# Attention followed by a tanhshrink FFN on one core: the conversion of the weights goes through PSUM tiles at the products with v

## The chip, the cores and the metric

The kernel runs on one core of a Trainium2 chip. The metric is device time in microseconds (us). Engines are named as in the profile: PE multiplies matrices and writes PSUM, PEld loads its weights, DVE, ACT and POOL work on elements, SP issues the DMA transfers. PSUM is the memory that PE writes its results to; SBUF is the other on-chip memory.

## The reference

The attention has 8 batches of 8 heads, 1152 positions and 64 numbers per head. The queries are averaged in twos, so 576 query rows meet 1152 keys. Its result, as 4608 tokens of 512 numbers, goes through a feed-forward network of 512 to 2048 to 512.

```python
q_pool = q.reshape(B, H, S // 2, 2, D).mean(axis=3)
scores = scale * np.matmul(q_pool, k.transpose(0, 1, 3, 2))
scores = scores - np.max(scores, axis=-1, keepdims=True)
attn = np.exp(scores)
attn = attn / (np.sum(attn, axis=-1, keepdims=True) + 1e-09)
x = np.matmul(attn, v)            # then (B, H, S, D) -> (4608, 512)
h = x @ w_in
out = (h - np.tanh(h)) @ w_out
```

q, k and v are 32-bit floats. The two weight matrices are 64-bit floats, and the kernel receives them as pairs of 32-bit words. It has to make 32-bit numbers of them before the network can use them: this is the conversion that the change is about.

## The kernel before

**Two stages.** The attention fills about the first half of the time and the network the second. The conversion of the weights is done during the attention, in 32 blocks of 128 x 512 weights, and its results go to DRAM, from where the network loads them.

**The attention.** Two heads make a pair, and there are 32 pairs. A pair takes U = 36 steps, called units, and is split in two halves of 18 units, 288 queries each. At each even unit of a half PE forms the scores of one of nine key tiles (`scores`: eight matmuls into one PSUM tile), and ACT takes the exponential out of it into a `p_f` tile. In a half's last unit PE multiplies the nine `p_f` tiles with v (`pv`, 36 matmul rows in the trace), and ACT copies the result out (`o_out`, tile `o_s`). After the products with v of the second half PE also sums the exponentials with a matrix of ones (`z_sums`, 32 rows), from `z` tiles that POOL has added up, and ACT copies that out too (`z_out`).

**The maxima.** While a pair's scores run, the row maxima of the next pair are found ahead: `max_part` has PE form 128 query rows by 384 keys for two heads, and one unit later DVE reduces them (`mx`). There are 15 of these per pair, eight in a second half and seven in a first half (counted by the half that runs beside them). At the end of a first half `max_rows` takes the maximum of these (`nm`), PE turns it (a transpose with `ident`), ACT and DVE split it in a high and a low part (`mt`), and it goes through DRAM to the rows `mb` of a matmul that subtracts it from the scores.

**High and low parts.** q and k are split too: `hi` (ACT, three instructions per pair) and `lo` (DVE, one subtraction over 128 x 1728), so that three products of parts stand for one product.

**The ring.** All PSUM tiles of the attention come from one pool of four (`banks`), each of 128 x 2 x 512 floats. A score tile, a `max_part` tile, the result of `pv` with that of `z_sums`, and the transpose each take one. PE can write a tile only when the reader of the tile that lay in that place before is done.

**The order** on each engine is the order in which the code calls it. Work that is not scores is put into tables by unit: `first` and `early` run at the start of a unit, ahead of its scores, and `at` behind its scores. In a half's last unit, `at` comes ahead of `pv`. So work in `at` of that unit and work in `first` of the next one stand on the two sides of `pv`, which matters only to PE and to what waits for PE.

**The conversion** of a block (`w_block`, called at unit 5 of a pair in the regular case) is: load (`w_raw`); ACT scales the upper words (`begin`); DVE clamps them, takes the sign, shifts and joins (three instructions); DVE takes the exponent (`w_2`), multiplies it with 16 bits of the lower word (two instructions); POOL adds; ACT makes the high part and POOL the low part (`w_hl`); SP stores. All tiles are in SBUF. The number ahead of each step is its unit behind the call.

In the profile most instructions of the attention have line L37, that of a helper that records every one of them, so they are told apart by their tiles: `w<-w` and `w<-w_raw,w` on DVE are the conversion, `mx<-ps` are the maxima, `lo<-kq,hi` is the low part.

Of the kernel before, what the change touches and what calls it, by code (L numbers as in the profile page):

```python
# [8 lines left out]
F32 = mybir.dt.float32  # L9
F32R = mybir.dt.float32r  # L10
I32 = mybir.dt.int32
# [32 lines left out]
def kernel(  # L44
# [18 lines left out]
    P = 128  # L63
# [76 lines left out]
    with ExitStack() as actx:  # L140
# [31 lines left out]
        def banks(dtype=F32):  # L172
            return ps_a.tile([P, 2, 512], dtype, name="ps")
# [173 lines left out]
        def w_block(u, kind, r, c):  # L347
# [7 lines left out]
            def begin():  # L355

                t[:] = [wp.tile([P, WB], I32, name=f"w_{i}", bufs=1 + (i < 2)) for i in range(3)]
                t.append(wp.tile([P, 2, WB], F32R, name="w_hl", bufs=2))
                act.activation(whole(t[0]), whole(hi), AF.Copy, scale=2.0 ** -112)

            def whole(x):
                return x.bitcast(F32)

            def store():
                src = t[3].bitcast(F32)
                if kind == 0:
# [3 lines left out]
                else:  # L370
                    sp.dma_start(wo_dram[r, :, :, c:c + WB], src)
            sp.dma_start(raw.rearrange("p n w -> p (n w)"),
                         (w_in, w_out)[kind][r * P:(r + 1) * P, 2 * c:2 * (c + WB)])
            for i, op in ((12, begin),
                          (30, lambda: ts(whole(t[0]), whole(t[0]), -top, top, op0=ALU.max, op1=ALU.min)),
                          (30, lambda: ts(t[1], t[0], -0x80000000, None, op0=ALU.bitwise_and)),
                          (48, lambda: stt(t[1], t[0], 3, t[1], op0=ALU.logical_shift_left, op1=ALU.bitwise_or)),
                          (48, lambda: ts(t[2], t[1], -0x800000, None, op0=ALU.bitwise_and)),
                          (48, lambda: stt(whole(t[2]), lo, 2.0 ** -36, whole(t[2]), op0=ALU.mult, op1=ALU.mult)),
                          (50, lambda: pool.tensor_tensor(whole(t[1]), whole(t[1]), whole(t[2]), op=ALU.add)),  # L380
                          (66, lambda: act.activation(t[3][:, 0], whole(t[1]), AF.Copy)),
                          (68, lambda: pool.tensor_tensor(t[3][:, 1], whole(t[1]), whole(t[3][:, 0]), op=ALU.subtract)),
                          (75, store)):
                add(u + i, op)
# [32 lines left out]
        for pi in range(n_pair):  # L417
            u = pi * U
            units = dict(load=-80, query_sums=-62, hi=-55, lo=-37, load_v=-30)
            row, steps = -19, (5, 11)  # L420
# [196 lines left out]
```

## Time and profile before

| what | value |
| --- | --- |
| median of the runs | 1643.94 us (three runs, 1643.39 to 1645.49) |
| the profiled execution | 1643.04 us |
| its span in the trace | 1641.3 us |
| TensorE clock granted | 0.999 of full speed |
| PE, DVE, ACT, POOL busy | 98%, 80%, 62%, 57% of the span |

The span is what lies between the first and the last instruction of the program; the profiled execution took 1.74 us more. A busy PE is not a PE at its peak, since matmuls overlap and their ends are modelled. Times in a timeline are from the start of the span. Each row of a timeline has the start, the time that the merged instructions took together, the engine, the line, the operation, the tiles and how many instructions were merged; in brackets stands how long the engine was idle ahead of it and what ended that wait.

### The profile page before, as it was taken

The numbers are of one execution on the slowest core, as the hardware profiler recorded it, in microseconds if no ns is written. First come the engines' busy times: TensorE is split into PE (matmuls) and PEld (weight loads), VectorE is DVE, ScalarE is ACT, GpSimd is POOL, SyncE is SP. The second block draws the span as 40 slices with busy tenths as digits, with TensorE's granted clock in tenths as the row PEclk, the third lists the DMA queues.
The fourth block names the chain that finished last, engine by engine and source line by source line (L and its number), as shares of the span: only waits on it lengthen the run. The fifth ranks groups of instructions, "written<-read, shape, count | busy, mean of one in ns | idle before, by whom it ended". The sixth has DMA issues, their size and how long they took to land.

```text
span 1641.3 us, 32231 instructions
## 1 busy us (share of the span) xinstructions
PE 1609.8 (98%) x12576; PEld 1245.2 (76%) x12576; DVE 1319.6 (80%) x1725; ACT 1023.9 (62%) x1865; POOL 942.9 (57%) x694
## 2 busy tenths in 40 slices
PE   5999999999999999999999999999999999999999
PEld 3667777777777777677778888888888888888898
DVE  7889888888898888888848677777777777777786
ACT  2655656556556565565566666666666666666786
POOL 2778778778787787877854343433434342423332
PEclk9999999999999999999999999999999999999999
DMA  3343444334433344343547110101011111000100
GB/s 141 120 138 108 126 127 136 125 108 138 135 115 125 121 141 126 108 130 133 183 146 268 39 36 21 48 26 52 26 47 31 39 39 39 26 33 20 32 22 27
DMA packets 72665, 147.86 MB, mean 90 GB/s; under 512 B 11136, under 2 KB 36672, under 8 KB 72512
## 3 DMA queue, kind: packets, MB, share of 16 engines
q1 hardware_dynamic: 72512, 145.80, 27.3%
q8 instruction: 99, 1.62, 0.4%
q14 instruction: 54, 0.44, 0.1%
HBM read 109.49 MB, written 36.27 MB: 89 GB/s over the span
## 4 chain that ended last, share of the span: by engine, by line
PE 85%; DVE 13%; issue 1%; ACT 0%; DMA 0%; DVEq 0%; ACTq 0%
PE ps L37 37%; PE ps_h L37 24%; PE ps_o L37 24%; DVE w L37 6%; DVE mx L37 6%; DVE nm L37 0%; DVE lo L37 0%; DMA q_n<-in_q_dram 0%; ACT hi L37 0%; DVE rec L37 0%; DVE kq L37 0%; ACT p_f L37 0%; DVEq L37 0%; ACT x L552 0%; ACT z_s L37 0%
## 5 line engine op out<-in xcount | busy, mean ns | idle before, releaser
L37 DVE TENSOR_REDUCE mx<-ps 128x2 f32<-128x768 f32 x480 | 434.3, 951 | 73.9 <-PE ps L37 73.7
L37 POOL TENSOR_TENSOR g_lo<-g_s,g_hi 128x512 fp32r<-128x512 f32 (+1 forms) x160 | 190.3, 1190 | 483.3 <-ACT g_hi L520 445.2
L37 ACT ACTIVATE p_f<-ps 128x576 f32<-128x576 f32 x576 | 361.7, 650 | 93.6 <-PE ps L37 79.3
L37 POOL TENSOR_TENSOR z<-p_f 128x576 f32<-128x576 f32 x192 | 280.0, 1459 | 154.1 <-ACT p_f L37 154.1
L37 PE MATMUL ps<-hi 64*128 64x288 f32 (+1 forms) x2112 | 316.7, 352 | 23.7 <-DVE mx L37 13.7
L37 PE MATMUL ps_h<-x,wi 128*128 128x512 f32 (+1 forms) x1440 | 318.3, 370 | 0.0
L37 PE MATMUL ps_o<-wo,g_hi 128*128 128x512 f32 x1008 | 311.5, 390 | 0.0
L37 PE MATMUL ps<-p_f,v 128*64 128x288 f32 x2304 | 293.5, 409 | 0.0
L37 PEld LDWEIGHTS ps_h<-x,wi 128*128 128x128 f32 x1440 | 253.1, 188 | 50.5
L37 PEld LDWEIGHTS ps<-hi 64*128 64x128 f32 x2112 | 194.4, 187 | 89.2 <-DVE mx L37 34.6
L37 PEld LDWEIGHTS ps<-p_f,v 128*64 128x64 f32 x2304 | 159.8, 137 | 113.7 <-ACT p_f L37 12.0
L509 ACT ACTIVATE g_u<-ps_h 128x512 f32<-128x512 f32 (+1 forms) x160 | 88.9, 556 | 236.3 <-PE ps_h L37 236.1
L514 DVE SCALAR_TENSOR_TENSOR ps_w<-g_u,ps_h 128x512 f32<-128x512 f32 (+1 forms) x160 | 103.1, 645 | 157.8 <-ACT g_t L510 157.2
L37 PEld LDWEIGHTS ps_o<-wo,g_hi 128*128 128x128 f32 x1008 | 187.6, 188 | 39.2
L37 POOL TENSOR_TENSOR z<-z,p_f 128x576 f32<-128x576 f32 x128 | 194.0, 1516 | 11.8 <-ACT p_f L37 1.9
L37 PE MATMUL ps_o<-wo,g_lo 128*128 128x512 f32 x504 | 196.2, 389 | 0.0
L37 PE MATMUL ps<-lo,hi 64*128 64x288 f32 x1152 | 170.8, 293 | 0.0
L37 PE MATMUL ps<-hi,lo 64*128 64x288 f32 x1152 | 170.7, 293 | 0.0
L37 PE MATMUL ps<-mb,ones_k 64*128 64x288 f32 x1152 | 170.2, 292 | 0.0
L37 ACT ACTIVATE o_s<-ps 128x288 f32<-128x288 f32 x64 | 26.3, 412 | 230.4 <-PE ps L37 230.4
L519 DVE COPY_PREDICATED g_s<-g_m,g_t 128x512 f32<-128x512 int32 (+1 forms) x160 | 115.0, 719 | 17.1 <-DVE g_s L518 0.9
L517 DVE SCALAR_TENSOR_TENSOR ps_w<-g_s,ps_w 128x512 f32<-128x512 f32 (+1 forms) x160 | 102.9, 643 | 16.6 <-DVE ps_w L516 0.5
(68 smaller groups left out, 2399.7 us busy)
## 6 DMA issues: line engine op xcount, KB each, us to landing
q_n<-in_q_dram SPq DMA_DIRECT2D x32, 576.0 KB
kq<-in_k_dram SPq DMA_DIRECT2D x32, 576.0 KB
v<-in_v_dram SPq DMA_DIRECT2D x32, 576.0 KB
x_dram<-o_s SPq DMA_DIRECT2D x32, 288.0 KB
out_dram<-o_s SPq DMA_DIRECT2D x34, 256.0 KB
w_raw<-in_moe_w_in_dram SPq DMA_DIRECT2D x16, 512.0 KB
wi_dram<-w_hl SPq DMA_DIRECT2D x16, 512.0 KB
w_raw<-in_moe_w_out_dram SPq DMA_DIRECT2D x16, 512.0 KB
```

Source lines behind the costliest of these rows:

```text
L37: ins = self.tc.keep_in_program_order(f(*args, **kwargs))
L509: nc.scalar.activation(u, h, AF.Square)
L514: nc.vector.scalar_tensor_tensor(w, u, -P0, h, op0=ALU.add, op1=ALU.mult)
L517: nc.vector.scalar_tensor_tensor(w, s2, P2, w, op0=ALU.add, op1=ALU.mult)
L519: last = nc.vector.copy_predicated(s1, m.bitcast(I32), th).ins
```

## The change

The conversion's first intermediate tile now lies in the PSUM ring instead of SBUF. `begin` on ACT writes a tile of the ring, and the clamp, the sign and the join on DVE read it; the joined word goes to the SBUF tile `w_1`. The exponent is written to a second tile of the ring (`scale`), and the multiplication with the lower word reads it from there. So each block takes two places of the ring, for a short time each. The tiles `w_0` are gone, `w_1` has three buffers instead of two, and the pair of tiles `w_hl` is taken only when the high part is made (`split`).

The steps also move. `begin`, the clamp, the sign and the join all stand in `first` of one unit, 31 behind the call: for a regular block that is the first unit of the next pair, right behind the products with v and the sums of a second half. The exponent and the multiplication stand in `first` 49 behind the call, right behind the products with v of that pair's first half. Before, `begin` stood ahead of the products with v of a first half, clamp and sign ahead of those of a second half, and join, exponent and multiplication ahead of those of the next first half. The low part `lo` moves by one unit, from the end of a second half to the first unit of the next pair, behind the scores there.

```diff
             def begin():
 
-                t[:] = [wp.tile([P, WB], I32, name=f"w_{i}", bufs=1 + (i < 2)) for i in range(3)]
-                t.append(wp.tile([P, 2, WB], F32R, name="w_hl", bufs=2))
+                t[:] = [banks(I32)[:, 0], wp.tile([P, WB], I32, name="w_1", bufs=3)]
                 act.activation(whole(t[0]), whole(hi), AF.Copy, scale=2.0 ** -112)
+
+            def scale():
+                t[0] = banks(I32)[:, 0]
+                ts(t[0], t[1], -0x800000, None, op0=ALU.bitwise_and)
+
+            def split():
+                t[0] = wp.tile([P, 2, WB], F32R, name="w_hl", bufs=2)
+                act.activation(t[0][:, 0], whole(t[1]), AF.Copy)
...
-            for i, op in ((12, begin),
-                          (30, lambda: ts(whole(t[0]), whole(t[0]), -top, top, op0=ALU.max, op1=ALU.min)),
-                          (30, lambda: ts(t[1], t[0], -0x80000000, None, op0=ALU.bitwise_and)),
-                          (48, lambda: stt(t[1], t[0], 3, t[1], op0=ALU.logical_shift_left, op1=ALU.bitwise_or)),
-                          (48, lambda: ts(t[2], t[1], -0x800000, None, op0=ALU.bitwise_and)),
-                          (48, lambda: stt(whole(t[2]), lo, 2.0 ** -36, whole(t[2]), op0=ALU.mult, op1=ALU.mult)),
-                          (50, lambda: pool.tensor_tensor(whole(t[1]), whole(t[1]), whole(t[2]), op=ALU.add)),
-                          (66, lambda: act.activation(t[3][:, 0], whole(t[1]), AF.Copy)),
-                          (68, lambda: pool.tensor_tensor(t[3][:, 1], whole(t[1]), whole(t[3][:, 0]), op=ALU.subtract)),
+
+            for i, op in ((31, begin),
+                          (31, lambda: ts(whole(t[0]), whole(t[0]), -top, top, op0=ALU.max, op1=ALU.min)),
+                          (31, lambda: ts(t[1], t[0], -0x80000000, None, op0=ALU.bitwise_and)),
+                          (31, lambda: stt(t[1], t[0], 3, t[1], op0=ALU.logical_shift_left, op1=ALU.bitwise_or)),
+                          (49, lambda: t.append(wp.tile([P, WB], I32, name="w_2", bufs=1))),
+                          (49, scale),
+                          (49, lambda: stt(whole(t[2]), lo, 2.0 ** -36, whole(t[0]), op0=ALU.mult, op1=ALU.mult))):
+                add(u + i, op, at=first)
+            for i, op in ((50, lambda: pool.tensor_tensor(whole(t[1]), whole(t[1]), whole(t[2]), op=ALU.add)),
+                          (66, split),
+                          (68, lambda: pool.tensor_tensor(t[0][:, 1], whole(t[1]), whole(t[0][:, 0]), op=ALU.subtract)),
                           (75, store)):
                 add(u + i, op)
...
-            units = dict(load=-80, query_sums=-62, hi=-55, lo=-37, load_v=-30)
+            units = dict(load=-80, query_sums=-62, hi=-55, lo=-36, load_v=-30)
```

**DVE, once around a pair.** The rows begin with the last seven maxima beside a second half and end with the maxima beside the next second half; `nm` marks the products with v of the first half. A number behind `w` is one tile of one block. Before:

```order
L37 TENSOR_REDUCE mx<-ps 128x2 x7
L37 TENSOR_TENSOR lo<-kq,hi 128x1728
L37 TENSOR_SCALAR w_2708<-w_2708 128x512
L37 TENSOR_SCALAR w_2709<-w_2708 128x512
L37 TENSOR_REDUCE mx<-ps 128x2 x7
L37 TENSOR_REDUCE nm<-mx 128x10
L37 SCALAR_TENSOR_TENSOR w_2709<-w_2708,w_2709 128x512
L37 TENSOR_SCALAR w_2710<-w_2709 128x512
L37 SCALAR_TENSOR_TENSOR w_2710<-w_raw,w_2710 128x512
L37 TENSOR_REDUCE mx<-ps 128x2
L37 TENSOR_TENSOR mt<-ps,mt 10x128
L37 TENSOR_REDUCE mx<-ps 128x2 x7
```

And with the change:

```order
L37 TENSOR_REDUCE mx<-ps 128x2 x7
L37 TENSOR_SCALAR ps<-ps 128x512
L37 TENSOR_SCALAR w_2927<-ps 128x512
L37 SCALAR_TENSOR_TENSOR w_2927<-ps,w_2927 128x512
L37 TENSOR_TENSOR lo<-kq,hi 128x1728
L37 TENSOR_REDUCE mx<-ps 128x2 x7
L37 TENSOR_REDUCE nm<-mx 128x10
L37 TENSOR_SCALAR ps<-w_2927 128x512
L37 SCALAR_TENSOR_TENSOR w_3108<-w_raw,ps 128x512
L37 TENSOR_REDUCE mx<-ps 128x2
L37 TENSOR_TENSOR mt<-ps,mt 10x128
L37 TENSOR_REDUCE mx<-ps 128x2 x7
```

The join (`w_2709<-w_2708,w_2709` before) has moved from the first half's products with v to those of the second half, and `lo` has moved behind the three instructions of the conversion. Between `nm` and the next maximum two instructions stand where there were three.

**ACT, over the same stretch.** Before:

```order
L37 ACTIVATE p_f<-ps 128x576 x8
L37 ACTIVATE w_hl<-w_2709 128x512
L37 ACTIVATE o_s<-ps 128x288
L37 ACTIVATE z_s<-ps 128x288
L37 ACTIVATE p_f<-ps 128x576 x9
L37 ACTIVATE hi<-kq 128x576 x3
L37 ACTIVATE w_3466<-w_raw 128x512
L37 ACTIVATE o_s<-ps 128x288
```

And with the change:

```order
L37 ACTIVATE p_f<-ps 128x576 x8
L37 ACTIVATE w_hl<-w_2927 128x512
L37 ACTIVATE ps<-w_raw 128x512
L37 ACTIVATE o_s<-ps 128x288
L37 ACTIVATE z_s<-ps 128x288
L37 ACTIVATE p_f<-ps 128x576 x9
L37 ACTIVATE hi<-kq 128x576 x3
L37 ACTIVATE o_s<-ps 128x288
```

`begin` (the row that reads `w_raw`) has moved from the first half's products with v to those of the second half, where DVE's next instruction now waits for it.

More of the change, by code (lines that the diff above doesn't have):

```diff
@@ L364, in store @@
             def store():
-                src = t[3].bitcast(F32)
+                src = t[0].bitcast(F32)
                 if kind == 0:
```

## The prediction

> **What bounds the kernel now.** I read the page first (busy shares, chain of waits), then the busy time by stage, then the timeline of DVE and PE around one pair, and last the pairs that are longer than the others. The chain's row by engine, and two stages of the table by windows (start and end, length, then busy us and count of PE, PEld, DVE, ACT, POOL, and the granted clock):
>
> ```profile
> PE 85%; DVE 13%; issue 1%; ACT 0%; DMA 0%; DVEq 0%; ACTq 0%
> ...
> 127.00:757.00 630.00, 625.47 (x6948) 452.25 (x6947) 559.35 (x586) 382.45 (x674) 502.40 (x324) 1.00 0.39 127
> ...
> 845.00:1641.00 796.00, 792.46 (x3647) 657.13 (x3645) 592.68 (x962) 530.81 (x996) 296.15 (x268) 1.00 0.16 51
> ```
>
> The network, from 845 us on, holds no conversion, and the change doesn't reach it. All that can move lies in the attention, where DVE is busy for 89% (559.35 of 630) and has 13% of the chain. So the question is where in a pair DVE is late. The products with v are clear marks in PE's timeline; three in a row, two of one pair and the first of the next:
>
> ```profile
> 298.76 4.59 PE L37 MATMUL ps<-p_f,v 128*64 128x288 f32 x36
> ...
> 310.75 4.59 PE L37 MATMUL ps<-p_f,v 128*64 128x288 f32 x36
> ...
> 324.00 4.59 PE L37 MATMUL ps<-p_f,v 128*64 128x288 f32 x36
> ```
>
> From the end of the first (303.35) to the second it takes 7.40 us, from the end of that (315.34) to the next pair 8.66. DVE over the same stretch:
>
> ```profile
> 299.98 0.18 DVE L37 TENSOR_REDUCE nm<-mx 128x10 f32<-128x30 f32 x1
> 300.08 0.68 DVE L37 SCALAR_TENSOR_TENSOR w<-w,w 128x512 int32<-128x512 int32 x1
> 300.87 1.45 DVE L37 TENSOR_SCALAR w<-w 128x512 int32<-128x512 int32 x1
> 302.36 1.77 DVE L37 SCALAR_TENSOR_TENSOR w<-w_raw,w 128x512 f32<-128x512 uint16 x1
> 304.05 0.94 DVE L37 TENSOR_REDUCE mx<-ps 128x2 f32<-128x768 f32 x1
> 305.41 0.28 DVE L37 TENSOR_TENSOR mt<-ps,mt 10x128 fp32r<-10x128 f32 x1 [0.41 <-ACT mt L37]
> 305.62 1.80 DVE L37 TENSOR_REDUCE mx<-ps 128x2 f32<-128x768 f32 x2
> ...
> 311.97 3.02 DVE L37 TENSOR_TENSOR lo<-kq,hi 128x1728 fp32r<-128x1728 f32 x1
> 314.91 1.96 DVE L37 TENSOR_SCALAR w<-w 128x512 f32<-128x512 f32 x2
> 317.83 0.96 DVE L37 TENSOR_REDUCE mx<-ps 128x2 f32<-128x768 f32 x1 [0.97 <-PE ps L37]
> ```
>
> The two sides differ. Beside the first half's products with v, the conversion runs until the first maximum, with no idle time between: DVE is just late. Beside the second half's, `lo` and two conversion instructions are done at 316.87, and DVE then waits 0.97 us for PE: there is slack. Behind a first half a delay is paid, behind a second half up to 0.97 us are free.
>
> How much a delay costs is seen where DVE has more to do. After each fourth pair the reciprocals of a batch stand behind the conversion; first PE, then DVE, then their count in the attention:
>
> ```profile
> 349.25 4.59 PE L37 MATMUL ps<-p_f,v 128*64 128x288 f32 x36
> ...
> 361.62 4.59 PE L37 MATMUL ps<-p_f,v 128*64 128x288 f32 x36
> ```
>
> ```profile
> 354.54 0.17 DVE L37 TENSOR_SCALAR rec<-rec 128x36 f32<-128x36 f32 x1
> 354.74 0.38 DVE L37 RECIPROCAL rec<-rec 128x36 f32<-128x36 f32 x1
> 355.04 0.90 DVE L37 TENSOR_REDUCE mx<-ps 128x2 f32<-128x768 f32 x1
> ```
>
> ```profile
> L37 DVE RECIPROCAL rec<-rec x7: 378/378/379, 152.0 to 760.2; 128x36 f32<-128x36 f32 x7
> ```
>
> Here the stretch is 361.62 - 353.84 = 7.78 us. And what it is with DVE free is seen in the first pair, where POOL happened to be idle (from 43.86, by its row), so that the conversion was quick; PE, DVE, POOL:
>
> ```profile
> 42.08 4.59 PE L37 MATMUL ps<-p_f,v 128*64 128x288 f32 x36
> ...
> 54.01 4.59 PE L37 MATMUL ps<-p_f,v 128*64 128x288 f32 x36
> ```
>
> ```profile
> 44.44 0.43 DVE L37 TENSOR_SCALAR w<-w 128x512 int32<-128x512 int32 x1
> 44.90 0.69 DVE L37 SCALAR_TENSOR_TENSOR w<-w_raw,w 128x512 f32<-128x512 uint16 x1
> 47.29 0.96 DVE L37 TENSOR_REDUCE mx<-ps 128x2 f32<-128x768 f32 x1 [1.69 <-PE ps L37]
> ```
>
> ```profile
> 45.68 1.27 POOL L37 TENSOR_TENSOR w<-w,w 128x512 f32<-128x512 f32 x1 [1.82 <-DVE w L37]
> ```
>
> DVE waited 1.69 us for PE, and the stretch was 54.01 - 46.67 = 7.34. These three numbers, 7.34, 7.40 and 7.78, are the core of the prediction. The same rows price the instructions: 0.43 and 0.69 us alone, 1.45 and 1.77 beside a busy POOL.
>
> **The change, part by part.** *First half.* Three instructions become two: the exponent into PSUM, and the multiplication that reads it from there. No conversion instruction of before touches PSUM, so their price is bounded: below by 0.43 (alone in SBUF), above by 1.77 (beside POOL). I take the nearest rows, those of the network that read and write PSUM over the same 512 elements, and for `lo` alone the row from the start of the kernel, when POOL was idle:
>
> ```profile
> L517 DVE SCALAR_TENSOR_TENSOR ps_w<-g_s,ps_w 128x512 f32<-128x512 f32 x125 | 87.1, 697 | 13.2 <-DVE ps_w L516 0.5
> ```
>
> ```profile
> 30.55 1.95 DVE L37 TENSOR_TENSOR lo<-kq,hi 128x1728 fp32r<-128x1728 f32 x1
> ```
>
> So 0.70 each, and 0.11 between two of which one needs the other (300.08 + 0.68 to 300.87). From 300.16 the two end at 301.67, with reciprocals (0.55) at 302.2, where PE's first maximum let DVE start no earlier than about 303.97 (in the first pair 0.62 us behind the products with v, 46.67 to 47.29). DVE is no longer late in either case, and every such stretch goes to 7.34. Cover: 1.8 us; if the two cost 1.45 and 1.77 as now, they end at 303.49 and regular pairs still gain, but those with reciprocals end at 304.04 and keep 0.06.
>
> A rule of the Trainium skill bears on this price, SBUF — State Buffer, section "Who interferes with whom": a DVE instruction with at most one input in SBUF, outside the two-port modes, doesn't contend with GpSimd (POOL). The trace agrees as far as it goes (0.43 and 0.69 alone against 1.45 and 1.77); by that rule the 0.70 holds beside POOL too, and the slower rival below loses its ground. Another, VectorE: DVE Perf Modes, section "Why PSUM operands drop a tier", speaks against the change: a PSUM operand loses the double rate of fp32. By it an instruction of 0.43 goes to 0.70, which over three is 0.8 us more per pair than alone. On the path that would be 24 us over 30 pairs and the change slower; against the 1.45 of now it is 2.2 less per pair, and the trace puts it under cover.
>
> *Second half.* Now three dependent conversion instructions come first and `lo` behind them, and they wait for `begin` on ACT, which is queued behind the high part `w_hl`. ACT and POOL there, the mean of `begin`, and a low part on POOL at a time when no `lo` ran:
>
> ```profile
> 311.27 0.62 ACT L37 ACTIVATE w_hl<-w 128x512 fp32r<-128x512 f32 x1
> ```
>
> ```profile
> L37 ACT ACTIVATE w<-w_raw 128x512 f32<-128x512 f32 x25 | 16.8, 673 | 0.0
> ```
>
> ```profile
> 313.12 3.00 POOL L37 TENSOR_TENSOR w_hl<-w,w_hl 128x512 fp32r<-128x512 f32 x1
> ```
>
> ```profile
> 99.45 1.46 POOL L37 TENSOR_TENSOR w_hl<-w,w_hl 128x512 fp32r<-128x512 f32 x1
> ```
>
> `begin` ends at 311.89 + 0.67 = 312.56; DVE's reductions end at about 312.05, so it waits 0.5 us. Then 3 x 0.70 + 2 x 0.11 = 2.32, to 314.88. POOL's low part, 1.46 long, is done at 314.58, so `lo` has POOL out of its way and costs 1.95: the end is 316.83, the maximum waits for PE until 317.83, and 1.0 us is spare. If `lo` still costs 3.02, the end is 317.90, 0.07 too late; over 29 pairs that is 2 us of loss. Queued behind `begin` on ACT are `o_s` and `z_s`, which need products that end 2.8 us later. I take no cost here, 0 to 2.
>
> *The ring.* Two more tiles per pair pass through four places. A place that `begin` took is free at 314.88, and one that the exponent took at 301.67; PE asks for its next score tiles only behind the products with v, after 315.34 and 303.35. Price nothing; without that cover, it would be the delay of the DVE instruction itself.
>
> *The long pairs.* Early blocks bunch up in the second and third pair. PE's marks there:
>
> ```profile
> 67.26 4.59 PE L37 MATMUL ps<-p_f,v 128*64 128x288 f32 x36
> ...
> 80.95 4.59 PE L37 MATMUL ps<-p_f,v 128*64 128x288 f32 x36
> ...
> 95.32 4.58 PE L37 MATMUL ps<-p_f,v 128*64 128x288 f32 x36
> ...
> 108.01 4.59 PE L37 MATMUL ps<-p_f,v 128*64 128x288 f32 x36
> ```
>
> The stretches are 9.10, 9.78 and 8.11 us, that is 1.76, 1.12 and 0.77 over 7.34, 8.66 and 7.34. Five conversion instructions stand at the first two, also with the change: 5 x 0.81 = 4.05 us, which fits beside 4.59 us of products only if `begin` is in time. It is behind three `hi` on ACT in the first, so I take 1.2 of 1.76; in the second 0.9 of 1.12, since `lo` follows; in the third, two instructions, all 0.77. At the start, before the first pair, the three instructions and `lo` take 2.3 + 1.95 to 3.0 us where `lo` and two slow ones take 4.95 (30.55 to 35.50): a gain of 0.7 to a loss of 0.4, taken as nothing.
>
> *The sum.* Thirty pairs have maxima beside their second half. Seven with reciprocals: 7 x 0.44 = 3.1. Three long ones: 1.2 + 0.9 + 0.77 = 2.9. The other twenty, without the first, which is at 7.34 already: 19 to 20 x 0.06 = 1.2. Together 7.2 us: 1643.04 - 7.2 = 1635.8 for a profiled execution. The median of the runs is 0.9 above that execution, so the prediction is 1636.7. From the bounds: at most 3.1 + 1.2 + 1.76 + 1.12 + 0.77 + 0.7 = 8.7; at least 3.1 + 1.2 + 0 + 0.4 + 0.77 - 2.0 - 0.4 = 3.1.
>
> DVE's work falls much more: its conversion from 1.96 + 0.68 + 1.45 + 1.77 = 5.9 to 3.5 us per pair, and `lo` by 1.1. Over 30 pairs that is 100 us, of which 7 count. Behind 7.34 and 8.66 stand PE's own matmuls and the chain of maxima, which the change doesn't shorten: 0.41 us before `mt` are a wait for ACT.
>
> **The rivals.** *Nothing follows.* The maximum at 304.05 is followed by a wait of 0.41 anyway, so its lateness might cost nothing, and the reciprocals might be paid elsewhere. Then only the long pairs gain, 2.9: 1641.0. The 7.78 next to 7.40 speaks against it.
>
> *Slower: the second half overruns.* The point is 317.83: from 312.56 there are 5.27 us for three instructions, two gaps and `lo`. With `lo` at 3.02 it decides from 0.68 per instruction on, with 1.95 from 1.03. Were PSUM to cost as much as the 768-element reduction (0.95) and POOL still to slow `lo`, the end would be 318.65, 0.8 late in 29 pairs: 23 us, against 7 gained: 1660. For it speaks that `lo` has run 3.02 beside POOL's low part; against it that POOL's would be done before.
>
> *More: a wait that vanishes.* The trace puts one kind of PE's waits ahead of a score or maximum tile on the conversion:
>
> ```profile
> PEld ps L37 <- issue: 24.3, 55, 0.5
> ...
> PEld ps L37 <- DVE w L37: 8.8, 19, 0.5
> ```
>
> If that is a true wait, 8.8 us in 25 pairs, 10 or so in all, go too: 1627. Against it: 55 + 19 are three per pair of one length, two of them called "issue", so this looks like the same gap at a change of operands.
>
> **How the numbers follow.** The forecast gets 0.78, nothing follows 0.10, slower 0.05, more 0.07. The range is 1633.5 to 1641.0: the bounds of the sum (1635.2 to 1640.8), about 1 us either way for the spread of the runs (1643.39 to 1645.49), cut at 1641.0. A measurement of this kernel can tell about 0.2%, 3.3 us, from no change, which is 1640.6. Faster: 0.78 + 0.07 = 0.85; the same: 0.10; slower: 0.05.
>
> **What would show it.** In the profile after: every regular stretch behind a first half at 7.34, also with reciprocals; an idle time ahead of the first maximum there of 1 us or more; 8.66 behind a second half; conversion instructions of 0.70, `lo` of 1.95, POOL's low part below 1.5; DVE busy about 100 us less in all. The prediction is wrong if the stretch of 8.66 grows (the first maximum of a pair without idle time ahead of it), if conversion instructions on PSUM take over 1 us, or if ACT's `o_s` or PE's first scores are late behind tiles of the ring.

## The result, and the profile after

The changed kernel takes 1635.13 us (median of five runs, 1634.2 to 1635.39); the kernel before took 1643.46 beside it (five runs, 1642.98 to 1645.49). The ratio is 0.9947, with a 95% interval of 0.9937 to 0.9958. The span of the profiled execution went from 1641.3 to 1632.4 us, and the last products with v of the attention start at 828.00 instead of 836.80: 8.8 of the 8.9 us lie in the attention.

The chain of waits by engine, and the same two stages by windows:

```profile
PE 97%; DVE 2%; ACT 0%; DMA 0%; issue 0%; ACTq 0%
...
127.00:757.00 630.00, 629.78 (x6977) 454.72 (x6975) 487.80 (x590) 383.48 (x676) 447.07 (x326) 1.00 0.40 127
845.00:1632.00 787.00, 783.62 (x3608) 650.40 (x3606) 588.01 (x955) 524.35 (x986) 295.62 (x268) 1.00 0.15 49
```

DVE is busy for 487.80 us in place of 559.35 in the attention's window, and its share of the chain is 2% instead of 13%. PE's timeline at the same pair as before, products with v only:

```profile
293.00 4.59 PE L37 MATMUL ps<-p_f,v 128*64 128x288 f32 x36
...
304.99 4.59 PE L37 MATMUL ps<-p_f,v 128*64 128x288 f32 x36
...
318.18 4.59 PE L37 MATMUL ps<-p_f,v 128*64 128x288 f32 x36
```

The stretch behind the first half is 304.99 - 297.59 = 7.40, as before; the one behind the second half 318.18 - 309.58 = 8.60, where it was 8.66. DVE's timeline over both:

```profile
298.21 0.96 DVE L37 TENSOR_REDUCE mx<-ps 128x2 f32<-128x768 f32 x1 [2.43 <-PE ps L37]
299.66 0.28 DVE L37 TENSOR_TENSOR mt<-ps,mt 10x128 fp32r<-10x128 f32 x1 [0.49 <-ACT mt L37]
...
306.72 0.70 DVE L37 TENSOR_SCALAR ps<-ps 128x512 f32<-128x512 f32 x1 [0.42 <-ACT ps L37]
307.45 0.69 DVE L37 TENSOR_SCALAR w<-ps 128x512 int32<-128x512 int32 x1
308.18 0.69 DVE L37 SCALAR_TENSOR_TENSOR w<-ps,w 128x512 int32<-128x512 int32 x1
308.78 1.95 DVE L37 TENSOR_TENSOR lo<-kq,hi 128x1728 fp32r<-128x1728 f32 x1
312.07 0.96 DVE L37 TENSOR_REDUCE mx<-ps 128x2 f32<-128x768 f32 x1 [1.34 <-PE ps L37]
```

Ahead of the first maximum DVE now idles 2.43 us behind a first half and 1.34 behind a second one. So it is late nowhere, and still the first stretch is 7.40 and not 7.34. That is the point at which the prediction failed, and most runs below are about it.

Here is where the 8.8 us came from, by the starts of all products with v. The start of the kernel: the first ones begin at 41.12 instead of 42.08, 0.96. The second pair: stretches of 7.59 and 8.61 in place of 9.11 and 9.78, 2.7. The third: 7.34 for 8.11, 0.8. The pairs with reciprocals: six go from 7.79 to 7.40 and a seventh from 8.01, 2.9. The other stretches behind second halves: 8.66 to 8.61 in nearly all, less 0.4 at two pairs that have 8.84 and 8.82, 1.4. The twenty regular stretches behind first halves: nothing.

### The profile page after: what moved, and what is told of

Same layout as the page of the kernel before. It is cut to its first block, busy times and chain, and to the rows that moved or that the text cites. A ratio compares the mean times of both kernels' runs of the same rounds, so it can differ in the third digit from the quotient of the medians.

```text
span 1632.4 us, 32106 instructions
## 1 busy us (share of the span) xinstructions
PE 1611.2 (99%) x12576; PEld 1246.3 (76%) x12576; DVE 1226.8 (75%) x1725; ACT 1023.4 (63%) x1865; POOL 873.3 (53%) x694
## 4 chain that ended last, share of the span: by engine, by line
PE 97%; DVE 2%; ACT 0%; DMA 0%; issue 0%; ACTq 0%
PE ps L37 49%; PE ps_h L37 24%; PE ps_o L37 24%; DVE mx L37 1%; DMA q_n<-in_q_dram 0%; ACT hi L37 0%; ACT p_f L37 0%; DVE lo L37 0%; DVE kq L37 0%; DVE w L37 0%; DVE ps L37 0%; ACT x L562 0%; ACT z_s L37 0%; ACT mt L37 0%; DVE nm L37 0%
## 5 line engine op out<-in xcount | busy, mean ns | idle before, releaser
L37 POOL TENSOR_TENSOR z<-p_f 128x576 f32<-128x576 f32 x192 | 275.2, 1433 | 236.7 <-ACT p_f L37 236.7
L37 POOL TENSOR_TENSOR z<-z,p_f 128x576 f32<-128x576 f32 x128 | 183.1, 1431 | 10.0
```

The lines of the kernel that those rows point to most:

```text
L37: ins = self.tc.keep_in_program_order(f(*args, **kwargs))
```

## The experiments

All runs in one table. A stretch is the time from the end of one half's products with v to the start of the next: regular pairs, pairs with reciprocals, and behind a second half. It is what most stretches of the kind have in the profiled execution; single ones differ. The ratio is to the kernel before beside the run, with its 95% interval.

| run | us | ratio | regular | reciprocals | second half |
| --- | --- | --- | --- | --- | --- |
| before | 1643.46 | | 7.40 | 7.79 | 8.67 |
| after | 1635.13 | 0.9947 (0.9937 to 0.9958) | 7.40 | 7.40 | 8.61 |
| e1_sbuf | 1640.09 | 0.998 (0.997 to 0.9989) | 7.40 | 7.40 | 8.67 |
| e2_scale | 1651.71 | 1.0047 (1.0032 to 1.0062) | 7.40 | 7.40, two of 7.63 and 7.68 | 9.05 |
| e3_lo | 1635.48 | 0.9949 (0.9934 to 0.9964) | 7.40 | 7.40 | 8.61 |
| e4_rec | 1641.01 | 0.9986 (0.9976 to 0.9995) | 7.40 | 7.40, two of 7.62 and 7.68 | 8.67 |
| e5_first | 1658.22 | 1.0083 (1.0067 to 1.0099) | 7.66 | 8.16 or 10.6 to 10.9 | 8.60 |
| e6_second | 1658.6 | 1.0091 (1.0076 to 1.0107) | 7.40 | 7.40 | 9.26 |
| e7_seen | 1632.31 | 0.9933 (0.992 to 0.9945) | 7.34 | 7.34 | 8.60 |
| e9_bseen | 1639.7 | 0.9975 (0.9964 to 0.9985) | 7.34 | 7.77 | 8.61 |
| e10_place | 1641.75 | 0.9988 (0.9979 to 0.9997) | 7.40 | 7.67, two of 7.90 and 7.94 | 8.67 |
| e8_seen2 | 1633.12 | 0.9934 (0.992 to 0.9947) | 7.34 | 7.34 | 8.61 |
| t_spot | 1634.01 | 0.9943 (0.9929 to 0.9957) | 7.38 | 7.38 | 8.60 |

### The order without PSUM, and PSUM without the order

**e1_sbuf**: the changed kernel with its two conversion tiles back in SBUF.

```diff
-                t[:] = [banks(I32)[:, 0], wp.tile([P, WB], I32, name="w_1", bufs=3)]
+                t[:] = [wp.tile([P, WB], I32, name="w_0", bufs=1), wp.tile([P, WB], I32, name="w_1", bufs=3)]
...
-                t[0] = banks(I32)[:, 0]
+                t[0] = wp.tile([P, WB], I32, name="w_3", bufs=1)
```

> The changed kernel with its order, but with both conversion tiles in SBUF again. Theory (the place counts: in PSUM the DVE instructions keep clear of POOL): beside POOL the five instructions go back to 0.7 to 1.8 us each and lo to 2 to 3 us; with three of them and lo behind the second half's products, the first maximum of a pair is late by 0 to 2.6 us, taken as 1.3, so 1635 + 29 x 1.3 = about 1673, and in any case over 1640. Rival (the new order alone makes the gain): 1635, the stretches stay at 7.40 and 8.61.

DVE's timeline in that run, from a first half's products to behind a second half's:

```profile
300.77 1.72 DVE L37 SCALAR_TENSOR_TENSOR w<-w_raw,w 128x512 f32<-128x512 uint16 x1
304.15 0.96 DVE L37 TENSOR_REDUCE mx<-ps 128x2 f32<-128x768 f32 x1 [1.65 <-PE ps L37]
...
312.68 2.37 DVE L37 TENSOR_SCALAR w<-w 128x512 f32<-128x512 f32 x2 [0.44 <-ACT w L37]
315.08 0.69 DVE L37 SCALAR_TENSOR_TENSOR w<-w,w 128x512 int32<-128x512 int32 x1
315.69 1.95 DVE L37 TENSOR_TENSOR lo<-kq,hi 128x1728 fp32r<-128x1728 f32 x1
318.01 0.96 DVE L37 TENSOR_REDUCE mx<-ps 128x2 f32<-128x768 f32 x1 [0.36 <-PE ps L37]
```

In SBUF the conversion is slower (1.72 for an instruction that takes 0.69 with PSUM), but it still fits: 1.65 and 0.36 us are idle. So neither theory held: the time is just over the 1640 of the first, but no maximum is late in a regular pair. By the medians the order alone gives 3.2 us (1643.33 beside it), mostly at the pairs with reciprocals (7.40) and at the third pair (7.40 for 8.11), and PSUM the other 5.

PSUM's part lies at the start and in the second pair, where blocks bunch up, and in 0.06 per second half. How much it is at the first two can't be read off this one execution (1641.44 us, above its kernel's median). The first products start at 42.69 against 41.12, and the second pair's stretches are 10.56 and 9.46 against 7.59 and 8.61. But in the second pair PE works at a granted clock of 0.60 for a while:

```profile
76.00:80.00 4.00, 3.92 (x36) 3.92 (x38) 2.22 (x5) 1.51 (x3) 1.88 (x2) 0.60 0.57 178
```

In the kernel before, at a clock of 1.00 there, DVE's first maximum is nearly as late (2.47 us behind the products, here 2.60), and the stretch is 9.11. So an estimated 1.3 of the 2.97 us go with the clock, and something at the start too, as told below.

**e4_rec**: the kernel before with only its reciprocals moved, from behind the conversion at a first half to the next second half.

```diff
-                    add(u + 17, lambda: reciprocals(dve, *tot[0]))
-                    add(u + 20, lambda: spread(sp, *tot.pop(0)))
+                    add(u + 35, lambda: reciprocals(dve, *tot[0]))
+                    add(u + 38, lambda: spread(sp, *tot.pop(0)))
```

> The kernel before, with the reciprocals moved from behind the first half's products to behind the second half's, where DVE waits 0.97 us for PE and they take 0.55. Theory: the stretches with reciprocals go from 7.78 to 7.40 and nothing else moves: 7 x 0.39 = 2.7 us less than before, about 1640.8. Rival (those stretches are long for another reason, such as the transfer of the sums): no change.

1641.01, with 7.40 at five of those seven pairs: as expected. (The fifth and the seventh have 7.68 and 7.62; why wasn't followed.) This prices the pairs with reciprocals by themselves. DVE is still late by about 0.1 us behind first halves: in a first half of this run the products end at 353.59 and the maximum starts 0.72 behind,

```profile
354.31 0.94 DVE L37 TENSOR_REDUCE mx<-ps 128x2 f32<-128x768 f32 x1
```

where one that waits for PE starts 0.62 behind (297.59 to 298.21 in the changed kernel). The stretch is 7.40 in both: the first 0.1 us costs nothing.

**e2_scale**: the kernel before, with only the exponent tile in PSUM; the order of the steps as before, so the tile is taken in `at`, ahead of the first half's products with v.

```diff
+            def scale():
+                t.append(banks(I32)[:, 0])
+                ts(t[4], t[1], -0x800000, None, op0=ALU.bitwise_and)
...
-                          (48, lambda: ts(t[2], t[1], -0x800000, None, op0=ALU.bitwise_and)),
-                          (48, lambda: stt(whole(t[2]), lo, 2.0 ** -36, whole(t[2]), op0=ALU.mult, op1=ALU.mult)),
+                          (48, scale),
+                          (48, lambda: stt(whole(t[2]), lo, 2.0 ** -36, whole(t[4]), op0=ALU.mult, op1=ALU.mult)),
```

> The kernel before, with only the exponent's tile in PSUM; order and everything else as before. Theory (the gain is the end of DVE's lateness behind a first half): the two instructions there go from 1.45 and 1.77 to 0.7 each, the seven stretches with reciprocals from 7.78 to 7.40 (2.7 us), the long third and second pairs lose 0.8 and about 1.5, the second halves stay at 8.66: about 1638.5. Rival (the second half's new order is needed for it): within 1 us of before, 1643.

It is slower than before, by 0.47%. The first halves gained about what was expected, but every stretch behind a second half grew by 0.38. PE, and DVE just ahead of it:

```profile
301.73 4.59 PE L37 MATMUL ps<-p_f,v 128*64 128x288 f32 x36 [0.32 <-DVE mx L37]
```

```profile
300.71 1.82 DVE L37 TENSOR_REDUCE mx<-ps 128x2 f32<-128x768 f32 x2 [0.33 <-PE ps L37]
```

The products with v wait for a maximum's reduction (the first of these two ends at about 301.6). With a tile of the ring taken just ahead of them, they get a place that is still held.

**e10_place** tests that reading: the same tile, but the two instructions stand in `first` of the next unit, where the change has them, so that the products take their place in the ring ahead of the exponent.

```diff
-                          (48, scale),
-                          (48, lambda: stt(whole(t[2]), lo, 2.0 ** -36, whole(t[4]), op0=ALU.mult, op1=ALU.mult)),
+            for op in (scale, lambda: stt(whole(t[2]), lo, 2.0 ** -36, whole(t[4]), op0=ALU.mult, op1=ALU.mult)):
+                add(u + 49, op, at=first)
```

> The kernel before, with the exponent tile in PSUM as in the run that was slower (ratio 1.0047), but its instruction and the multiplication behind it written in the place where the change has them, so that the tile is taken from the ring behind the products with v and not ahead of them; DVE's order stays. Theory (what cost 0.38 per pair was the place in the ring: the first half's products then took the place of a maximum that DVE had not read yet): stretches behind a second half back to 8.67, those behind the pairs with reciprocals still at 7.40; 2.5 us less than before: about 1640.8. Rival (a fifth user of the four places costs 0.38 wherever it is taken): 1651 to 1652, stretches of 9.05.

8.67 again: the 0.38 was the place in the ring. In the program, the first matmul of these products waits for DVE in the one and for ACT's exponential in the other:

```
L37 MATMUL ps<-p_f,v 64x288 [waits DVE_49]
L37 MATMUL ps<-p_f,v 64x288 [waits Activation_49]
```

The pairs with reciprocals only went to 7.67, not 7.40, so it is 0.9 us slower than expected. There the maximum isn't late (354.43 to 355.05, 0.62), but `mt` waits longer for ACT, 0.76 against 0.49 in the changed kernel.

```profile
354.28 0.69 DVE L37 SCALAR_TENSOR_TENSOR w<-w_raw,ps 128x512 f32<-128x512 uint16 x1
355.05 0.96 DVE L37 TENSOR_REDUCE mx<-ps 128x2 f32<-128x768 f32 x1
356.77 0.28 DVE L37 TENSOR_TENSOR mt<-ps,mt 10x128 fp32r<-10x128 f32 x1 [0.76 <-ACT mt L37]
```

```profile
355.02 0.18 PEld L37 LDWEIGHTS ps<-hi 64*128 64x128 f32 x2 [0.27 <-DVE w L37]
```

```profile
355.94 0.65 ACT L37 ACTIVATE p_f<-ps 128x576 f32<-128x576 f32 x1 [1.05 <-PE ps L37]
```

This is the ring again. DVE, behind the reciprocals, reads the exponent's tile until 354.28 + 0.69 = 354.97, and PE's next scores wait 0.27 us for that place. The exponential, with `mt` behind it on ACT, starts 1.51 us behind the products instead of 1.24, and the stretch is 0.27 longer. So a tile that is taken behind the products is free only while DVE is done with it in time.

**e3_lo**: the changed kernel with `lo` back at the end of the second half, ahead of the conversion.

```diff
-            units = dict(load=-80, query_sums=-62, hi=-55, lo=-36, load_v=-30)
+            units = dict(load=-80, query_sums=-62, hi=-55, lo=-37, load_v=-30)
```

> The changed kernel with the low part lo ahead of the conversion again, as before. Theory: lo runs beside POOL again and takes 2 to 3 us where it takes 1.95, and the idle time of 1.34 us ahead of a pair's first maximum shrinks by that, but stays above zero: the time stays at 1635 to 1636. Rival (lo's place is part of the gain): 1638 or more, first maxima without idle time ahead.

`lo` takes 3.0 us again, since POOL's low part runs beside it and itself takes 2.9 (1.29 on average in the changed kernel), and the stretches stay the same:

```profile
L37 DVE TENSOR_TENSOR lo<-kq,hi 128x1728 fp32r<-128x1728 f32 x32 | 94.4, 2951 | 0.0
```

```profile
L37 POOL TENSOR_TENSOR w_hl<-w,w_hl 128x512 fp32r<-128x512 f32 x32 | 92.7, 2898 | 0.0
```

So the move of `lo`, by which it takes 1.95, is worth nothing in regular pairs: that microsecond lies in DVE's slack. Only in the second pair, where two blocks meet, does it count: 9.01 for 8.61.

### How much lateness costs, on both sides

**e5_first** and **e6_second** make DVE late in the changed kernel, by repeats that don't alter the result.

```diff
-                ts(t[0], t[1], -0x800000, None, op0=ALU.bitwise_and)
+                for _ in range(5):
+                    ts(t[0], t[1], -0x800000, None, op0=ALU.bitwise_and)
```

> The changed kernel, with the exponent instruction of the conversion written five times in a row (the result is the same), so that DVE has four more instructions of about 0.77 us (0.70 and the gap), 3.08 us, ahead of the first maximum behind a first half's products with v, where it idles 2.43 us now. Theory (what DVE is late there is paid, but for a first 0.1 to 0.2 us; the late reciprocals of the kernel before, 0.59 late, cost 0.39): 0.65 late, some 0.45 per pair in 29 pairs, 13 us, and about 2.6 in the crowded second pair: about 1651, stretches of 7.85 in place of 7.40. Rival (lateness behind a first half isn't paid, and the gain at the pairs with reciprocals has another cause): 1635, stretches of 7.40.

```diff
-                          (31, lambda: ts(t[1], t[0], -0x80000000, None, op0=ALU.bitwise_and)),
+                          *[(31, lambda: ts(t[1], t[0], -0x80000000, None, op0=ALU.bitwise_and))] * 4,
```

> The changed kernel, with the sign instruction written four times in a row (the result is the same): three more of about 0.73 us, 2.19, ahead of the first maximum behind a second half's products, where DVE idles 1.34 us now. This is the price and the point of the prediction's slower rival. Theory (the second half overruns once its 1.34 are used up): 0.85 late, 0.65 to 0.85 of it paid in 29 pairs, 19 to 25 us: 1654 to 1660, stretches of 9.3 to 9.45 in place of 8.61. Rival (the second half's maxima are not on the path, and slack there has no bound): 1635 to 1637.

Lateness is paid, on both sides. **e6_second** shows it plainly; PE's products behind a second half, and DVE's first maximum behind them:

```profile
318.54 4.59 PE L37 MATMUL ps<-p_f,v 128*64 128x288 f32 x36
```

```profile
326.35 1.81 DVE L37 TENSOR_REDUCE mx<-ps 128x2 f32<-128x768 f32 x2
```

The maximum starts 326.35 - 323.13 = 3.22 us behind the products, where it is 2.49 in the changed kernel (309.58 to 312.07): 0.73 late here and 0.75 in most pairs (0.85 were meant). The stretch is 9.26 for 8.60, 0.66 longer. Over 29 pairs that is 19 us. The rest of the loss lies at the start (first products at 44.31) and in the second pair (10.49 and 10.13), partly at a lower clock (0.50 granted from 38 to 44 us).

DVE in **e5_first**, with five exponent instructions:

```profile
304.44 3.60 DVE L37 TENSOR_SCALAR ps<-w 128x512 int32<-128x512 int32 x5
308.13 0.69 DVE L37 SCALAR_TENSOR_TENSOR w<-w_raw,ps 128x512 f32<-128x512 uint16 x1
308.73 0.95 DVE L37 TENSOR_REDUCE mx<-ps 128x2 f32<-128x768 f32 x1
```

The products end at 307.72, so the maximum is 308.73 - 307.72 - 0.62 = 0.39 late (not 0.65: one takes 0.72 with its gap, not 0.77), and the stretch is 0.26 longer. This can't be put down to the maximum alone. The ring's places fall otherwise in this run: PE's first scores wait for `o_s`,

```profile
308.22 0.19 PEld L37 LDWEIGHTS ps<-hi 64*128 64x128 f32 x2 [0.19 <-ACT o_s L37]
```

and the exponential starts 1.43 us behind the products instead of 1.24. In the kernel before, where the exponential is on time, 0.1 of lateness costs nothing (regular pairs), 0.58 costs 0.39 (reciprocals) and 0.86 costs 0.71 (third pair). So some 0.1 to 0.2 us are free, and the rest is paid in full. The total of 1658.22 is above the expected 1651 for two reasons: the second pair (9.44 and 10.87), and three of the pairs with reciprocals, told of at the end. One of the four executions took 1652.4, at a granted clock of 1.000; the others took 1657.37 to 1659.68, at 0.997.

### The 0.06 us of the regular pairs

After the first results the regular stretch had DVE out of the way and was still 7.40. What differs between the first pair (7.34) and the others is ACT. The first scores' exponential behind a first half's products starts 1.24 us behind their end in regular pairs (297.59 to 298.83), before and after; in the first pair 1.18. In the program it waits for two counters, PE's and ACT's own (for the `p_f` buffer's last use, twelve earlier), and in the first pair, where that buffer is new, for PE's alone. First pair, then a regular one, and the first scores behind a second half in the changed kernel (there `begin` has already waited for ACT's counter, because of its place in the ring):

```
L37 ACTIVATE p_f<-ps 128x576 [waits PE_49]
L37 ACTIVATE p_f<-ps 128x576 [waits PE_49,Activation_49]
L37 ACTIVATE p_f<-ps 128x576 [waits PE_49] x2
```

So the theory became: an exponential on the path that has to wait for a second counter starts 0.06 us later. It explains the 7.40 and the 8.66 to 8.61 at once.

**e7_seen**: the changed kernel with a copy of one column on ACT ahead of each products with v, which reads the last exponential and so takes that wait.

```diff
+                seen = sm.tile([P, 2], F32, name="seen")
+                act.activation(seen[:, 0:1], hf.p[-1][:, 0, 0:1], AF.Copy)
                 pv(u, hf)
```

> The changed kernel, with one tiny copy on ACT (128x1) ahead of each products with v, that reads the last exponential of the half just done and so takes ACT's wait for its own earlier work. By the program's waits the exponentials behind it then wait for PE alone, where they now wait for PE and for ACT itself. Theory (an exponential that waits for two counters starts 0.06 us later than one that waits for one, and this is the 0.06 between 7.34 and 7.40): stretches behind a first half 7.34 or a little less, those behind a second half 8.55 to 8.61, 1.5 to 4 us less in all: 1631 to 1633.5. Rival (the 0.06 has another cause, such as the state of PE's queue or of the buffers): stretches of 7.40 and 8.61, 1635; or more, if the copy itself delays ACT.

PE's products and ACT in that run:

```profile
292.79 4.59 PE L37 MATMUL ps<-p_f,v 128*64 128x288 f32 x36
...
304.71 4.59 PE L37 MATMUL ps<-p_f,v 128*64 128x288 f32 x36
```

```profile
295.06 0.19 ACT L37 ACTIVATE seen<-p_f 128x1 f32<-128x1 f32 x1
297.43 0.41 ACT L37 ACTIVATE o_s<-ps 128x288 f32<-128x288 f32 x1 [2.18 <-PE ps L37]
298.55 0.65 ACT L37 ACTIVATE p_f<-ps 128x576 f32<-128x576 f32 x1 [0.71 <-PE ps L37]
```

against ACT in the changed kernel:

```profile
297.63 0.41 ACT L37 ACTIVATE o_s<-ps 128x288 f32<-128x288 f32 x1 [2.00 <-PE ps L37]
298.83 0.65 ACT L37 ACTIVATE p_f<-ps 128x576 f32<-128x576 f32 x1 [0.78 <-PE ps L37]
```

The exponential starts 298.55 - 297.38 = 1.17 us behind the products, not 1.24, and the stretch is 304.71 - 297.38 = 7.33, and so in every regular pair; the two stretches of 8.8 are gone as well. It takes 1632.31 us, five runs of 1632.18 to 1632.59, all below the changed kernel's lowest, 1634.2 (the two were not run side by side, and their intervals overlap at the edge), and its last products start 2.04 us earlier, at 825.96: a version that beats both kernels.

**e9_bseen**: the kernel before with the same copy, which tells ACT's wait from DVE's lateness, since DVE is still late by 0.1 there.

> The kernel before, with the same tiny copy on ACT ahead of each products with v, and nothing else of the change. Theory (the 0.06 per stretch is the exponential's second wait, on both sides of a pair; what DVE is late in a regular pair costs nothing): regular stretches 7.40 to 7.34, the pairs with reciprocals 7.79 to about 7.79 or 7.73, the stretches behind a second half 8.67 to 8.61; some 50 stretches by 0.06, 3 us less: about 1640.3. Rival (behind a first half DVE's lateness of 0.09 counts in the regular pairs, as the prediction said): 7.40 stays there, 8.61 only behind the second half: about 1641.7.

Regular stretches of 7.34 and second halves of 8.61: the theory's numbers, also in the total (1639.7 for 1640.3). So none of the difference between 7.40 and 7.34 was DVE's.

The same shows without a copy. In the third pair of the changed kernel the program has this exponential wait for PE alone: it starts 1.18 us behind the products, and the stretch is 7.34. In e1_sbuf it waits for both there, starts 1.24 behind, and the stretch is 7.40. Behind second halves it starts 3.10 us behind the products before and 3.04 after.

**e8_seen2** adds a copy that reads POOL's partial sum too, so that nearly all exponentials wait for PE alone.

```diff
+                act.activation(seen[:, 1:2], hf.zs[1][:, 0, 0:1], AF.Copy)
```

> The changed kernel with the tiny copy ahead of each products with v (1632.3, stretches of 7.34 and 8.60), and with a second one that reads POOL's second partial sum of that half, so that nearly all exponentials wait for PE alone. Theory (only a wait on the path to the next product counts, and the later exponentials of a half aren't there, PE being busy throughout): stretches of 7.34 and 8.60, 1632 to 1633. Rival (each second wait costs, wherever it stands): three exponentials per half, up to 0.06 each, 60 halves: down to 1622.

No further gain in the regular stretches: only a wait on the path to the next products counts. The 0.8 us above e7_seen lie mostly in the second pair (8.38 for 7.69), where the second copy waits 0.51 us for POOL and holds up `begin` behind it.

**t_spot**: the changed kernel with one of a second half's maxima moved to just ahead of the products with v, which puts its reduction beside them.

```diff
-            spots = [x for half, us in ((-54, (2, 4, 8, 10, 12, 14, 16)), (-36, (2, 4, 8, 10, 14, 16)))
+            spots = [x for half, us in ((-54, (2, 4, 8, 10, 14, 16, 17)), (-36, (2, 4, 8, 10, 14, 16)))
```

> The changed kernel, with one of the seven maxima beside a second half moved from behind that half's first scores to just ahead of its products with v (the units 2, 4, 8, 10, 14, 16, 17 in place of 2, 4, 8, 10, 12, 14, 16), so that its reduction (0.96 us) falls beside the products, where DVE idles 1.34 us now. Theory (DVE has room there, and PE and the ring have one maximum less to pass between two products): about the same or up to 0.3 us less per pair: 1626 to 1636. Rival (the ring's order decides: the products with v, or the scores behind them, then wait for the place that this reduction holds): 0.4 us more per pair, as when the exponent's tile stood ahead of the products: about 1647.

The time is that of the changed kernel within the intervals. The maximum's matmuls stay in the same stretch (the expectation has that wrong); what leaves it is 0.95 us of DVE, and the stretch goes from 7.40 to 7.38. But two things changed in it. The ring's places fall otherwise, and in the program the exponential now waits for PE alone: it starts 1.17 us behind the products, by which the stretch would be 7.34. And the products at its end now wait for a maximum's reduction, where they wait for ACT's exponential in the changed kernel:

```profile
306.73 1.40 PEld L37 LDWEIGHTS ps<-p_f,v 128*64 128x64 f32 x13 [0.23 <-DVE mx L37]
```

That is the rival's mechanism, at a price of some 0.04 us.

## Why the prediction was right, and where it was not

**The whole.** Forecast 1636.7, measured 1635.13. The sum was 7.2 us and 8.9 came (by the spans), so the time is right, but several of its parts were not; that it came so near is partly luck. The lower end of the range, 1633.5, is 0.7 below what its working gives (1635.2 less 1).

**The step that failed** is "The other twenty ... x 0.06 = 1.2", with its ground that DVE is "just late" in regular pairs (304.05 for 303.97) and "every such stretch goes to 7.34". The mechanism was wrong, not the size: the first pair's 7.34 was put down to DVE being free there, while it is due to buffers that nobody had used before. Lateness of 0.1 costs nothing (e4_rec, e9_bseen), and the 0.06 go with ACT's second wait (e7_seen).

**A gain that the sum didn't have** is the same 0.06 behind the second halves, where "8.66" was to stay: 1.4 us. It came from a place in the ring that makes `begin` wait first. The two errors are of about the same size and cancel.

**The pairs with reciprocals**: 3.1 forecast, 2.9 measured, and e4_rec gives 2.3 for them alone (a ratio of 0.9986). This was right; of the 0.44 per pair, 0.39 is what the change took away, and the rest stays with ACT's second wait.

**The long pairs**: 1.2 + 0.9 + 0.77 forecast, 1.52 + 1.17 + 0.77 measured. Right in kind, and the first two mis-sized low: DVE waits for `begin` only 0.17 us at the second pair. By e1_sbuf PSUM is what counts at the second pair, though part of its loss there goes with the clock, and the order alone at the third (7.40).

**The start**: taken as nothing, between -0.4 and +0.7; it is a gain of 0.96, outside these bounds. The three instructions and `lo` take from 30.51 to 34.44, where the best case was 4.25 us, so the term was mis-sized at its best end:

```profile
30.51 0.69 DVE L37 TENSOR_SCALAR ps<-ps 128x512 f32<-128x512 f32 x1
31.24 0.69 DVE L37 TENSOR_SCALAR w<-ps 128x512 int32<-128x512 int32 x1
31.96 0.69 DVE L37 SCALAR_TENSOR_TENSOR w<-ps,w 128x512 int32<-128x512 int32 x1
32.57 1.95 DVE L37 TENSOR_TENSOR lo<-kq,hi 128x1728 fp32r<-128x1728 f32 x1
34.44 2.68 DVE L37 TENSOR_REDUCE mx<-ps 128x2 f32<-128x768 f32 x3
```

PE waits there for the first of these maxima, before and after:

```profile
36.50 0.61 PE L37 MATMUL ps<-hi 64*128 64x288 f32 x2 [3.66 <-DVE mx L37]
```

```profile
35.45 0.61 PE L37 MATMUL ps<-hi 64*128 64x288 f32 x2 [0.77 <-DVE mx L37]
```

That is 1.05 us. When the first products start depends on one thing more, which differs between executions: behind this wait two matmuls take 0.44 us at first, and 0.30 from some point on. That point is at about 38.6 in the changed kernel, 39.6 before, 40.7 in e4_rec, which has the same order as before up to there, and 41.5 in e1_sbuf. So the first products start between 40.83 and 41.92 in the traces of the changed kernel, e3_lo, e5_first, e7_seen and e8_seen2, at 42.69 in t_spot, and between 42.08 and 43.60 in those of the kernel before, e2_scale, e4_rec, e9_bseen and e10_place.

**The prices** were right: 0.70 per instruction, `lo` 1.95, a wait of 0.42 for `begin` (0.5 forecast); only the gap between two is 0.03 for 0.11. The cover behind the second half is 1.34 us for 1.0. By the rule of the Trainium skill, SBUF — State Buffer, "Who interferes with whom", an instruction with at most one input in SBUF, outside the two-port modes, doesn't contend with POOL. The trace agrees: the sign and the join take 0.69 in the changed kernel while POOL's low part runs,

```profile
307.36 1.27 POOL L37 TENSOR_TENSOR w_hl<-w,w_hl 128x512 fp32r<-128x512 f32 x1
```

and the multiplication with both inputs in SBUF 1.72 in e1_sbuf. By the Trainium skill, VectorE: DVE Perf Modes, "Why PSUM operands drop a tier", a PSUM operand loses the double rate of fp32. The trace agrees, 0.69 for the 0.43 of the quick instruction, and that lies in the slack. DVE's work fell by 559.35 - 487.80 = 71.6 us in 25 pairs, 86 in 30, where 100 was forecast.

**The rivals.** "Nothing follows" is ruled out by the pairs with reciprocals. The slower one did not occur, but its mechanism is real: past the slack, e6_second pays 0.66 per pair for 0.75 of lateness, where the forecast of 23 us counted all of it. What the prediction didn't have is the loss of e2_scale: "price nothing" for the ring holds for the place that the change takes, a place one unit earlier costs 0.38 per pair, and even this place costs 0.27 where DVE is done with the tile too late (e10_place, at the pairs with reciprocals). The vanishing wait was none: the gap that was called "DVE w" 19 times and "issue" 55 times is now

```profile
PEld ps L37 <- issue: 33.5, 75, 0.5
```

that is, the same three per pair (25 pairs) and of the same length.

**Open.** Two stretches of 8.84 and 8.82 in the changed kernel, at the thirteenth and sixteenth pair, are there in three other runs of its order too (e3_lo, e5_first, e6_second) and gone in e7_seen, e8_seen2 and t_spot; their cause wasn't found.

## What to carry to other kernels

Where DVE has slack, a slower conversion in SBUF does as well as a fast one in PSUM; what counts is which place in the order is paid for, and in a ring of tiles, who takes the place behind whom. An edit elsewhere can change that (e5_first and t_spot), so it has to be looked up in the program of each run. Before a small difference between a first pass and the later ones is put down to an engine's load, compare what the instruction on the path waits for in each: a first pass has new buffers, and so fewer waits. Where an instruction on the path waits for two engines, a tiny earlier instruction on the same engine can take one of the waits while there is time.

## What the runs showed of the hardware

A second counter to wait for costs an exponential on ACT 0.06 to 0.07 us of start, though that counter was reached long before (1.24 against 1.17 us behind the products). The Trainium skill, Perfetto Trace Analysis, "Identifying Dependency Chains", says that an instruction which waits for several engines may get an extra instruction ahead of it with the further waits. It names no time. The program has that instruction here: it waits for PE's counter, and the exponential behind it for ACT's own. The timelines don't show it, so whether the 0.06 us are its own time is open.

PE's clock falls behind some short waits. In e5_first, at the ninth pair, PE waited 1.80 us for DVE, until 257.01; DVE is so late at this and two further pairs with reciprocals because the first instruction of these takes 1.21 to 1.32 us there, for 0.17 at others. Three windows, and a group of matmuls ahead of the wait and behind it:

```profile
248.00:256.00 8.00, 7.21 (x67) 4.39 (x63) 7.17 (x11) 4.63 (x9) 5.51 (x4) 1.00 0.42 138
256.00:262.00 6.00, 4.99 (x50) 4.78 (x50) 4.45 (x7) 2.66 (x6) 4.08 (x3) 0.72 0.41 140
262.00:268.00 6.00, 6.00 (x62) 4.28 (x62) 5.51 (x8) 3.64 (x6) 5.45 (x5) 1.00 0.16 63
```

```profile
254.79 0.29 PE L37 MATMUL ps<-hi,lo 64*128 64x288 f32 x2
...
257.66 0.44 PE L37 MATMUL ps<-hi,lo 64*128 64x288 f32 x2
```

The granted clock is 0.72 over six microseconds, and two matmuls take 0.44 us where they take 0.29 at full clock. The stretch is 10.58, against 8.16 at other pairs with reciprocals. Behind waits of 1.52 and 1.80 at the two further pairs the same is seen, and behind one of 1.98 in e1_sbuf, but not behind one of 1.77 at the second pair of e5_first, nor behind one of 1.84 in the kernel before: length alone doesn't decide it. The granted clock doesn't show every slow stretch either: in e4_rec two matmuls take 0.44 us from 36.9 to 40.7, at a granted clock of 1.00. What sets the clock wasn't found.
